# Linear attention and a GELU MLP on one core: outputs and state products of two chunks at a time, instead of outputs of four and states of four

## The chip, the cores and the metric

The kernel runs on one core of a Trainium2 chip. The core has five engines that work side by side and wait for each other through semaphores: TensorE (PE in the profile; PEld is its weight load), VectorE (DVE), ScalarE (ACT), GpSimd (POOL) and SyncE (SP), which here issues DMA transfers. The metric is the device time in microseconds (us), the median of several runs. The profile is of one execution.

## The reference

There are two stages. The first is linear attention with decay, over 4 batches, 8 heads, 768 positions and head dimension 64, in blocks of 64 positions:

```python
for b in range(nb):
    intra = einsum('bhic,bhjc->bhij', qb, kb) * Dmask          # lam ** (i - j), lower triangle
    intra = einsum('bhij,bhjd->bhid', intra, vb)
    inter = einsum('bhid,bhde->bhie', qb * lam_pow, kv_state)   # what earlier blocks left
    out[:, :, sl] = intra + inter
    kv_state = lam_block * kv_state + einsum('bhsd,bhse->bhde', kb * rev_pow, vb)
```

The second takes the attention's output as 3072 tokens of 512 features and computes gelu(x @ w_in) @ w_out, with 2048 hidden features and the exact GELU. Inputs and outputs are float32.

## The kernel before

The kernel computes in bf16 with float32 accumulation. It cuts the sequence into chunks of 128 positions, so there are 6 chunks for each of 4 batches, 24 in all. Chunk n belongs to batch n % 4 and to place n // 4 in the sequence. The four chunks of one place are a group; groups are numbered 0 to 5.

For one chunk the attention has these parts:

- `dma_transposes` (lines 184 to 190) gets the transposed k (`kT`) and q (`qT`). SP issues two transposing DMAs; POOL multiplies q by its decay (`q_hat`) between them. `request` calls it.
- `decay_k` (line 165) gives `k_dec`, k times the decay, on POOL.
- `scores` (line 192) makes 8 products of 64x128 weights on TensorE into two PSUM banks, and DVE multiplies them by the mask into `sc_m`.
- `inter` (line 220) makes 4 products of the carried state with `qT`, into the bank `o_ps`.
- `intra` (line 227) adds 8 products with weights of 128x64, two for each pair of heads, into the same bank. Then `o_ps` is copied to the group's tile `x_t`, from group 2 on by DVE.
- `next_state` (line 203) makes 4 products of `k_dec` and v into a bank `kv_ps`. DVE adds the old state (`tmp`, line 216) and multiplies by the decay (`state`, line 217). `take_state` makes that the current state. Group 5 has none.

The MLP of group g needs the x_t of all four of its chunks. It is a list of blocks, each of four products of 512 columns on TensorE: 16 blocks of the first product (`mm1`, line 263, 17 in group 1, where the last chunk's columns of the first four are a block of their own), with GELU on ACT, and then 16 blocks of the second (`mm2`, line 275), four for each chunk. After each chunk's fourth block ACT copies the sum to `o_sb` and SP sends it out (lines 280 and 281).

While the MLP of group g runs, the attention of group g + 1 is computed by visits to TensorE between the blocks. The dictionary `visits` says ahead of which block a visit stands. For groups 1 to 4 the loop at line 433 fills it in. For group g the chunks visited begin at n = (g + 1) * 4:

- `pair_a(n)` and `pair_a(n + 2)`: the scores of two chunks each, ahead of blocks a0 and a1.
- `quad_b(n)`: inter of four chunks, then intra of four, ahead of block b.
- `kv(n, ..., n + 3)`: the state products of four, ahead of block st.
- `requests(m)`: transposes and `k_dec` of chunks m and m + 1, and the loads of chunks m + 2 and m + 3.

The schedule is manual: every engine carries out its instructions in the order in which the code issues them, and waits only for data and for buffers. So `requests` takes no time on TensorE, and where it stands matters for what lies ahead of it on the queues of SP (output transfers and transposes) and of POOL (`q_hat`, `k_dec` and the issue of loads).

The tag "sc" has four PSUM banks, used in turn for scores, `o_ps` and `kv_ps`. The tag "m" has the other four, for the MLP. Chunks of q, k and v have 12 buffers each, `kT`, `qT`, `q_hat` and `sc_m` 6, `k_dec` 8, `o_sb` 6, `x_t` 2.

Of the kernel before, what the change touches and what calls it, by code (L numbers as in the profile page):

```python
# [9 lines left out]
BF16 = mybir.dt.bfloat16  # L10
# [5 lines left out]
def kernel(  # L16
# [12 lines left out]
    B, H, S, D = q.shape  # L29
# [10 lines left out]
    M = B  # L40
    NG = NB
# [7 lines left out]
    work_pool = ctx.enter_context(tc.tile_pool(name="work", bufs=6))  # L49
# [104 lines left out]
    live = {}  # L154

    def bank(shape, dtype, tag, name):
        return ps.tile(shape, dtype, tag=tag, name=name, bufs=4)
# [7 lines left out]
    def decay_k(c, eng):  # L165

        if c.so < NB - 1:
            c.k_dec = work_pool.tile([128, H, D], BF16, tag="kd", name="k_dec", bufs=8)
            eng.tensor_mul(c.k_dec, c.k, lam_m[:, :, None].to_broadcast((128, H, D)))  # L169

    def transposes(c, between=lambda: None):
# [20 lines left out]
    def scores(c):  # L192
        sc_ps = [bank([128, HP, C], F32, "sc", f"sc_ps{hi}") for hi in range(2)]
        for hp in range(HP):
            for hi in range(2):
                p = slice(hi * D, (hi + 1) * D)
                nc.tensor.matmul(sc_ps[hi][:, hp, :], c.kT[p, hp, :], c.qT[p, hp, :], start=True, stop=True)  # L197
        c.sc_m = work_pool.tile([128, HP, 2, C], BF16, tag="sc_m", name="sc_m")
        dmask_r = dmask.rearrange("p (hp hi) i -> p hp hi i", hi=2)
        for hi in range(2):  # L200
            nc.vector.tensor_mul(c.sc_m[:, :, hi, :], sc_ps[hi], dmask_r[:, :, hi, :])  # L201

    def next_state(c):

        if c.so == NB - 1:
            return
        kv_ps = bank([128, HP, 128], F32, "sc", "kv_ps")
        for hp in range(HP):
            nc.tensor.matmul(kv_ps[:, hp, :], c.k_dec[:, 2 * hp:2 * hp + 2, :], c.v[:, 2 * hp:2 * hp + 2, :],  # L209
                             start=True, stop=True)  # L210
        new = state_pool.tile([128, HP, 128], BF16, tag=f"state{c.b}", name="state")
        if c.so == 0:
            nc.vector.tensor_mul(new, kv_ps, lam_blk)
        else:
            tmp = state_pool.tile([128, HP, 128], F32, tag="tmp", name="tmp")
            nc.vector.tensor_add(tmp, kv_ps, states[c.b])  # L216
            nc.vector.tensor_mul(new, tmp, lam_blk)  # L217
        c.after = new

    def inter(c):  # L220
        c.o_ps = bank([128, HP, C], F32, "sc", "o_ps")
        if c.so > 0:
            for hp in range(HP):
                nc.tensor.matmul(c.o_ps[:, hp, :], states[c.b][:, hp, :], c.qT[:, hp, :],  # L224
                                 start=(hp == 0), stop=False, skip_group_check=True)

    def intra(c):
        for hp in range(HP):
            for hi in range(2):
                nc.tensor.matmul(c.o_ps[hi * D:(hi + 1) * D, hp, :], c.v[:, 2 * hp + hi, :], c.sc_m[:, hp, hi, :],  # L230
                                 start=(c.so == 0 and hp == 0), stop=True, skip_group_check=True)
        x_o = xT[c.so][:, :, c.b * C:(c.b + 1) * C]
        if c.so < 2:
            nc.scalar.copy(x_o, c.o_ps)
        else:
            nc.vector.tensor_copy(x_o, c.o_ps)  # L236
# [5 lines left out]
    def take_state(c):  # L242

        if c.so < NB - 1:
            states[c.b] = c.after
# [109 lines left out]
    for n in range(M):  # L355
        decay_k(live[n], nc.vector)
# [9 lines left out]
    def request(n):  # L366
        begin(n)
        dma_transposes(live[n])
# [3 lines left out]
    def prefetch(upto):  # L372
        while next_load[0] <= min(upto, NCH - 1):
            for name in "kqv":
                load(next_load[0], name)
            next_load[0] += 1

    def kv(*ns):
        for n in ns:
            next_state(live[n])  # L380
            take_state(live[n])

    def first_requests():
        for n in (2 * M, 2 * M + 1):
            request(n)
        for n in range(M, 2 * M):
            decay_k(live[n], nc.gpsimd)
        prefetch(2 * M + 3)
        for n in (2 * M, 2 * M + 1):
            decay_k(live[n], nc.gpsimd)  # L390
# [20 lines left out]
    def pair_a(n):  # L411
        for c in (live[n], live[n + 1]):
            scores(c)

    def quad_b(n):
        quad = [live[n + i] for i in range(M)]
        for c in quad:
            inter(c)
        for c in quad:
            intra(c)  # L420

    def requests(n):
        for m in (n, n + 1):
            request(m)
        for m in (n, n + 1):
            decay_k(live[m], nc.gpsimd)
        prefetch(n + 3)

    def add(g, i, f):
        visits.setdefault((g, i), []).append(f)  # L430


    for g in range(1, NG - 1):
        n = (g + 1) * M
        a0, a1, b, st = {1: (10, 22, 27, 31), 2: (6, 19, 25, 30)}.get(g, (5, 14, 21, 28))
        if g == 1:
            add(g, a0 - 2, lambda n=n: requests(n + 2))
        add(g, a0, lambda n=n: pair_a(n))
        add(g, a1, lambda n=n: pair_a(n + 2))
        if g + 2 < NG:  # L440
            add(g, a1 + 1, lambda n=n: requests(n + M))
            add(g, b + 1, lambda n=n: requests(n + M + 2))
        add(g, b, lambda n=n: quad_b(n))
        add(g, st, lambda n=n: kv(n, n + 1, n + 2, n + 3))

    for g in range(NG):
        if g + 1 < NG:
# [34 lines left out]
```

## Time and profile before

| what | us |
|---|---|
| median of 8 runs | 213.59 (213.04 to 214.54) |
| the profiled execution, its own time | 213.01 |
| its span, first to last instruction | 211.2 |
| PE busy | 205.9 |
| ACT / POOL / DVE busy | 87.3 / 102.8 / 75.8 |

The span lies inside the execution's own time, which is 1.8 us longer. A matmul's recorded length overlaps with the next one's, so busy time of PE says that it had work, not how much it got done; for that, start times are compared. The profile's first table gives busy time by engine, and a later one the chain of work that ended last. "L275" is line 275 of the kernel. In a time line, rows that follow each other on one engine with the same line are merged, and "x16" is their number.

### The profile page before, as it was taken

To read this page: it belongs to the slowest core of one execution; us is meant where nothing else is said; L and a number is where in the kernel's file an instruction comes from. 1 tells how busy PE (TensorE), PEld (TensorE's weight loads), DVE (VectorE), ACT (ScalarE), POOL (GpSimd) and SP (SyncE) were. 2 spreads that over 40 slices of the span, in tenths; PEclk is the share of its full clock that TensorE was granted. 3 is DMA by queue.
4 is the path that set the end of the run, shared out by engine and by line. 5 is a ranking of instruction groups with operands and counts; after the bars stand their busy time and mean duration, and the time that the engine had idled before them with its cause. 6 is when DMAs were issued, how large, how long until landed. Compare 5 with 4: busy or idle time off the path is not lost.

```text
span 211.2 us, 3570 instructions
## 1 busy us (share of the span) xinstructions
PE 205.9 (97%) x1472; PEld 105.5 (50%) x1472; DVE 75.8 (36%) x122; ACT 87.3 (41%) x153; POOL 102.8 (49%) x118
## 2 busy tenths in 40 slices
PE   7999999999999999999999999999999999999994
PEld 2545754556644455444465444455444464444442
DVE  3768130175393136740414842244542240000000
ACT  5674662326646111556211565311465311566121
POOL 7994533892997947949695295761000000000000
PEclk9999999999999999999999999999999999999999
DMA  7999999999999699999999969999400012100112
GB/s 86 134 158 197 206 207 188 155 209 154 179 91 117 78 164 111 145 129 175 98 150 116 160 140 147 111 161 119 149 0 0 3 50 99 50 3 0 50 50 99
DMA packets 100799, 24.48 MB, mean 116 GB/s; under 512 B 92976, under 2 KB 97840, under 8 KB 100784
## 3 DMA queue, kind: packets, MB, share of 16 engines
q0 software_dynamic: 78592, 13.51, 85.9%
q1 hardware_dynamic: 22192, 10.76, 25.1%
q8 instruction: 11, 0.18, 0.4%
q14 instruction: 4, 0.03, 0.1%
HBM read 27.27 MB, written 6.29 MB: 159 GB/s over the span
## 4 chain that ended last, share of the span: by engine, by line
PE 90%; DVE 5%; ACT 2%; DMA 1%; issue 1%
PE o_ps L275 38%; PE h_ps L263 38%; PE o_ps L230 3%; PE sc_ps L197 3%; PE o_ps L224 2%; PE kv_ps L209 2%; PE o_ps L289 2%; PE t_ps L176 2%; DVE state L217 1%; DMA lam_b<-in_lam_dram 1%; DVE tmp L216 1%; DVE sc_m L201 1%; PE idle_ps L324 1%; DVE qT L182 1%; ACT lam_q L132 1%
## 5 line engine op out<-in xcount | busy, mean ns | idle before, releaser
L263 PE MATMUL h_ps<-x_t,w_in_t 128*128 128x512 bf16 (+2 forms) x432 | 86.2, 356 | 0.0
L275 PE MATMUL o_ps<-w_out_t,g_t 128*128 128x512 bf16 x368 | 82.9, 379 | 0.0
L265 ACT ACTIVATE g_t<-h_ps 128x512 bf16<-128x512 f32 (+1 forms) x99 | 57.8, 584 | 34.0 <-PE h_ps L263 33.8
L263 PEld LDWEIGHTS <-w_in_t 128*128 128x128 bf16 x432 | 39.4, 98 | 41.6 <-DMA w_in_t<-in_moe_w_in_dram 0.3
L275 PEld LDWEIGHTS <-g_t 128*128 128x128 bf16 x368 | 35.0, 98 | 40.8
L201 DVE TENSOR_TENSOR sc_m<-sc_ps,dmask 128x512 bf16<-128x512 f32 x48 | 30.0, 683 | 41.2 <-PE sc_ps L197 41.2
L280 ACT COPY o_sb<-o_ps 128x512 f32<-128x512 f32 x23 | 13.5, 586 | 73.2 <-PE o_ps L275 73.2
L189 POOL TENSOR_TENSOR q_hat<-q_t,lam_p 128x512 bf16<-128x512 bf16 x16 | 17.2, 1073 | 28.4 <-issue 15.8
L66 POOL DMA_DIRECT2D k_t<-in_k_dram x24 | 22.1, 919 | 6.5 <-DMA w_in_t<-in_moe_w_in_dram 4.0
L66 POOL DMA_DIRECT2D q_t<-in_q_dram x24 | 21.6, 899 | 3.5 <-DMA w_out_t<-in_moe_w_out_dram 3.4
L66 POOL DMA_DIRECT2D v_t<-in_v_dram x23 | 20.8, 908 | 3.3 <-DMA w_out_t<-in_moe_w_out_dram 1.6
L236 DVE CAST x_t<-o_ps 128x512 bf16<-128x512 f32 x16 | 9.9, 684 | 18.1 <-PE o_ps L230 18.1
L169 POOL TENSOR_TENSOR k_dec<-k_t,lam_m 128x512 bf16<-128x512 bf16 x16 | 16.3, 1048 | 0.0
L216 DVE TENSOR_TENSOR tmp<-kv_ps,state 128x512 f32<-128x512 f32 x16 | 11.0, 685 | 12.4 <-PE kv_ps L209 12.4
L324 PE MATMUL idle_ps<-idle 128*128 128x512 bf16 x32 | 11.5, 476 | 1.2 <-DVE idle L105 1.2
L217 DVE TENSOR_TENSOR state<-tmp,lam_blk 128x512 bf16<-128x512 f32 x16 | 11.9, 746 | 0.6
L182 DVE TENSOR_TENSOR qT<-t_ps,lam_q 128x512 bf16<-128x512 bf16 x8 | 5.5, 690 | 14.9 <-PE t_ps L176 14.0
L197 PE MATMUL sc_ps<-qT,kT 64*128 64x128 bf16 x192 | 8.2, 217 | 0.8 <-DVE qT L182 0.4
L197 PEld LDWEIGHTS <-kT 64*128 64x128 bf16 x192 | 5.7, 94 | 6.4 <-issue 4.1
L230 PE MATMUL o_ps<-sc_m,v_t 128*64 128x128 bf16 x192 | 7.9, 222 | 0.2
L230 PEld LDWEIGHTS <-v_t 128*64 128x64 bf16 x192 | 5.8, 109 | 2.8 <-issue 1.6
L181 ACT COPY kT<-t_ps 128x512 bf16<-128x512 bf16 x8 | 4.7, 589 | 5.1 <-PE t_ps L176 5.1
(41 smaller groups left out, 71.6 us busy)
## 6 DMA issues: line engine op xcount, KB each, us to landing
out_dram<-o_sb SPq DMA_DIRECT2D x23, 256.0 KB, 2.3
k_t<-in_k_dram POOLq DMA_DIRECT2D x24, 128.0 KB, 4.6
q_t<-in_q_dram POOLq DMA_DIRECT2D x24, 128.0 KB, 5.7
v_t<-in_v_dram POOLq DMA_DIRECT2D x23, 128.0 KB, 6.6
w_out_t<-in_moe_w_out_dram POOLq DMA_DIRECT2D x4, 512.0 KB, 16.8
w_in_t<-in_moe_w_in_dram POOLq DMA_DIRECT2D x2, 512.0 KB, 11.3
w_in_t<-in_moe_w_in_dram POOLq DMA_DIRECT2D x2, 384.0 KB, 7.8
v_f<-in_v_dram SPq DMA_DIRECT2D x1, 256.0 KB, 3.6
```

Of the source, the lines that this page charges most:

```text
L66: nc.gpsimd.dma_start(raw[n, name], chunk_of(name, n))
L169: eng.tensor_mul(c.k_dec, c.k, lam_m[:, :, None].to_broadcast((128, H, D)))
L189: nc.gpsimd.tensor_mul(q_hat, c.q, lam_p[:, :, None].to_broadcast((128, H, D)))
L197: nc.tensor.matmul(sc_ps[hi][:, hp, :], c.kT[p, hp, :], c.qT[p, hp, :], start=True, stop=True)
L201: nc.vector.tensor_mul(c.sc_m[:, :, hi, :], sc_ps[hi], dmask_r[:, :, hi, :])
L217: nc.vector.tensor_mul(new, tmp, lam_blk)
L230: nc.tensor.matmul(c.o_ps[hi * D:(hi + 1) * D, hp, :], c.v[:, 2 * hp + hi, :], c.sc_m[:, hp, hi, :], start=(c.so == 0 and hp == 0), stop=T ...
L263: nc.tensor.matmul(h_ps[:, f, :], w, x_t[:, ki, lo:hi], start=(ki == 0 and f == 0), stop=(ki == NK1 - 1), skip_group_check=True)
L265: nc.scalar.activation(g_t[:, kf:kf + n_kf, lo:hi], h_ps, ACT.Gelu)
L275: nc.tensor.matmul(om[io], g_t[:, kf, io * C:(io + 1) * C], w_out_t[:, kf, :], start=(kf == 0), stop=(kf == NK2 - 1))
L280: nc.scalar.copy(o_sb, om[io])
L324: nc.tensor.matmul(idle_ps[0], idle[:, :128], idle, start=True, stop=True)
```

## The change

`quad_b` becomes `pair_b`. For two chunks it issues inter, then the state products, then intra and the taking over of the state. The separate kv visit is gone. Each group now has four visits in the order scores, `pair_b`, scores, `pair_b`, at the blocks (10, 15, 21, 27) in group 1 and (4, 10, 18, 26) in groups 2 to 4. Requests stand two blocks ahead of the first scores and one block after the first `pair_b`. `k_dec` takes the pool's 6 buffers instead of 8. The visits of group 0, the first ones of group 1 (up to block 7), the MLP and the loads of the weights are as they were.

```diff
     def decay_k(c, eng):
         if c.so < NB - 1:
-            c.k_dec = work_pool.tile([128, H, D], BF16, tag="kd", name="k_dec", bufs=8)
+            c.k_dec = work_pool.tile([128, H, D], BF16, tag="kd", name="k_dec")
...
-    def quad_b(n):
-        quad = [live[n + i] for i in range(M)]
-        for c in quad:
+    def pair_b(n):
+        pair = live[n], live[n + 1]
+        for c in pair:
             inter(c)
-        for c in quad:
+        for c in pair:
+            next_state(c)
+        for c in pair:
             intra(c)
+            take_state(c)
...
     for g in range(1, NG - 1):
         n = (g + 1) * M
-        a0, a1, b, st = {1: (10, 22, 27, 31), 2: (6, 19, 25, 30)}.get(g, (5, 14, 21, 28))
-        if g == 1:
-            add(g, a0 - 2, lambda n=n: requests(n + 2))
+        a0, b0, a1, b1 = (10, 15, 21, 27) if g == 1 else (4, 10, 18, 26)
+        add(g, a0 - 2, lambda n=n: requests(n + 2))
         add(g, a0, lambda n=n: pair_a(n))
+        add(g, b0, lambda n=n: pair_b(n))
+        if g + 2 < NG:
+            add(g, b0 + 1, lambda n=n: requests(n + M))
         add(g, a1, lambda n=n: pair_a(n + 2))
-        if g + 2 < NG:
-            add(g, a1 + 1, lambda n=n: requests(n + M))
-            add(g, b + 1, lambda n=n: requests(n + M + 2))
-        add(g, b, lambda n=n: quad_b(n))
-        add(g, st, lambda n=n: kv(n, n + 1, n + 2, n + 3))
+        add(g, b1, lambda n=n: pair_b(n + 2))
```

## The prediction

> **What bounds the kernel now.** I read the page first, then the stretches by group, then TensorE in order of time.
>
> ```profile
> span 211.2 us, 3570 instructions
> PE 205.9 (97%) x1472; PEld 105.5 (50%) x1472; DVE 75.8 (36%) x122; ACT 87.3 (41%) x153; POOL 102.8 (49%) x118
> PEclk9999999999999999999999999999999999999999
> PE 90%; DVE 5%; ACT 2%; DMA 1%; issue 1%
> ```
>
> TensorE is busy for 97% of the span, at full clock in all slices, and makes up 90% of the chain that ended last. Busy matmuls overlap, so this could hide slack. The table by stretch (groups 1 and 2 with the seams before them; its length comes after the stretch, then PE's busy time) says that there is next to none:
>
> ```profile
> 50.00:85.60 35.60, 35.47 (x293) 19.07 (x291) 17.59 (x27) 13.84 (x25) 28.72 (x31) 1.00 1.39 128
> 85.60:117.40 31.80, 31.80 (x225) 15.98 (x224) 12.66 (x21) 11.90 (x20) 23.17 (x25) 1.00 1.58 135
> ```
>
> Group 1's stretch has 0.13 us of idle, group 2's none. So what decides is how long each visit holds TensorE, and whether the new places make it wait. The time line of TensorE gives the first (start, length, line; the next row's start minus its own is what a row really holds the engine):
>
> ```profile
> 47.06 0.61 PE L224 MATMUL o_ps<-qT,state 128*128 128x128 bf16 x8
> 47.60 0.64 PE L230 MATMUL o_ps<-sc_m,v_t 128*64 128x128 bf16 x16
> 48.17 0.40 PE L197 MATMUL sc_ps<-qT,kT 64*128 64x128 bf16 x8
> ...
> 136.90 1.06 PE L224 MATMUL o_ps<-qT,state 128*128 128x128 bf16 x16
> 137.89 1.08 PE L230 MATMUL o_ps<-sc_m,v_t 128*64 128x128 bf16 x32
> 138.90 6.22 PE L275 MATMUL o_ps<-w_out_t,g_t 128*128 128x512 bf16 x28
> 144.96 1.06 PE L209 MATMUL kv_ps<-v_t,k_dec 128*128 128x128 bf16 x16
> 145.85 3.62 PE L275 MATMUL o_ps<-w_out_t,g_t 128*128 128x512 bf16 x16
> ```
>
> inter (L224): 8 hold 0.54, 16 hold 0.99: 0.45 per 8, and 0.09 fixed, paid on going over to intra. State products (L209): 16 hold 0.89, twice that 0.45 with nothing fixed. intra (L230): 16 hold 0.57, 32 hold 1.01: 0.44 per 16, and 0.13 fixed, paid on going in and back out to full-width products. So every change from full-width (128*128) to half-width weights (128*64) and back costs 0.22 us, and while it lasts nothing else runs on TensorE. An MLP product holds 6.06/28 = 0.216 us, a block of four 0.866.
>
> **The change, part by part.** (1) Each of groups 1 to 4 has one quad_b (16 inter, 32 intra) and, in groups 1 to 3, one kv visit of 16. It gets two pair_b, each 8 inter, 8 state products, 16 intra. No matmul is added. Before: 0.99 + 1.01 + 0.89 = 2.89 us per group, of which 0.22 is one change of width. After: the same streaming, 2.67, with two changes, 3.11. Group 4 has no state products: 2.00 becomes 2.22. The kv visit that disappears gives nothing back, since it had no fixed cost. Sum: 4 x 0.22 = +0.88 us, all on the path, since TensorE has no idle time to put it in. The going over from state products to intra is in no row. Its bounds: 0 if the state products in between hide it (0.09 less in each of 8 pair visits, 0.72 less in all), above the dearest change that the rows show, 0.13 (8 x 0.04 = 0.32 more). I take 0.09, since the state products have the form of inter (128*128, 128x128).
>
> Here the Trainium skill may be weighed. "TensorEngine Tiling (Array Packing)", section Key Properties, says that changing the tiling mode drains the TensorE, which the 0.22 us agrees with; it speaks against this change. With the drain of about 175 ns that "TensorE: Matmul & The Clock Gate", section Single matmul latency, gives, eight more changes (four in, four out) would be an estimated 1.4 us. The rows' 0.88 stands, since they have the same products.
>
> (2) DVE. Per pair its queue gets tmp, state, tmp, state, then the two copies to x_t, where before the copies came alone and the state work later.
>
> ```profile
> 57.11 1.23 DVE L217 TENSOR_TENSOR state<-tmp,lam_blk 128x512 bf16<-128x512 f32 x1
> ...
> 138.34 2.48 DVE L236 CAST x_t<-o_ps 128x512 bf16<-128x512 f32 x4 [5.13 <-PE o_ps L230]
> 145.38 0.69 DVE L216 TENSOR_TENSOR tmp<-kv_ps,state 128x512 f32<-128x512 f32 x1 [4.55 <-PE kv_ps L209]
> ...
> 146.72 0.68 DVE L216 TENSOR_TENSOR tmp<-kv_ps,state 128x512 f32<-128x512 f32 x1
> ```
>
> The first tmp starts 0.42 after its state products (145.38 against 144.96), so 0.87 into the visit; a chunk's tmp and state take 1.34 (146.72 - 145.38); the four copies took 2.48, 0.62 each. The last copy ends 0.87 + 2.68 + 1.24 = 4.8 us into the visit. Who waits for it: the scores that need the o_ps banks, and for the second pair the next group's first MLP product, which reads x_t. Both come 6 blocks after the visit at the earliest: 1.56 + 6 x 0.866 = 6.76. Slack 1.96, cost nothing. The cover thins where POOL multiplies beside it: the L217 at 57.11 took 1.23 instead of 0.69. With both slow the copy ends at 5.9, slack 0.9.
>
> The page "SBUF — State Buffer", section Who interferes with whom, goes further: a DVE instruction with two SBUF inputs and a GpSimd one that reads SBUF block each other fully. With a whole k_dec (1.05) behind each state, an estimate by it is 4.8 + 2.1 = 6.9 and a stall of 0.15 at a seam, at most 0.6 over four; no row shows more than 1.23.
>
> (3) New earliest dates for data. In group 1, block 10's products resume at 62.16, so b0 (block 15) begins at 62.16 + 5 x 0.866 = 66.49, its state products 0.45 later at 66.94; a1 begins at 66.49 + 6.76 = 73.25.
>
> ```profile
> 63.04 2.09 POOL L169 TENSOR_TENSOR k_dec<-k_t,lam_m 128x512 bf16<-128x512 bf16 x2
> ...
> 68.83 1.19 SPq L190 DMA_TRANSPOSE qT<-q_hat  x1
> ```
>
> ```profile
> qT<-q_hat SPq DMA_TRANSPOSE x1, 2.4
> ```
>
> k_dec of chunks 8 and 9 is done at 65.13, 1.8 us ahead; the last qT for a1 (issued 68.83, landed 2.4 later, the DMA view of that stretch) is there at 71.2, 2.0 ahead. Nothing on POOL's queue moves: its instructions keep their order. k_dec with 6 buffers instead of 8 waits for the state products of six chunks earlier: chunk 10's (POOL at 68.22) for chunk 4's, done by 57; chunk 14's (93.94) for chunk 8's, about 67.5; later ones have as much. Cost nothing.
>
> (4) SP's queue. The requests for chunks 12, 16 and 20 move ahead of a group's four output transfers, those for 14, 18 and 22 behind all four. The moved-back ones are the risk. Request 14 stands behind the out of group 1's last block (copied at 85.84 by ACT); its first transpose went out only at 87.59 before, so nothing changes. Request 18 can start at about 118; four transposes of 1.3 us each are issued by 123.2, and with the slowest landing that the kT row has (9.2) are there at 132.4, for a visit at 117.8 + 18 x 0.866 + 2.1 = 135.5. Request 22: 150.2, 155.4, 164.6, against 167.7. The moved-ahead ones hold outputs back (group 1's first, ready at 72.5, until 83.4); at most three pile up, for six buffers. Cost nothing. The loads of w_in are not in the diff: nothing.
>
> Sum against the profiled execution: 213.01 + 0.88 = 213.89. The median of the runs is 0.58 above that execution, so the forecast is 214.47, 0.41% more.
>
> **Rivals.**
> A: a new wait beside it. POOL's q_hat waited 3.30 and 1.09 us for loads before the k_dec of chunks 8 and 9, so these follow DMA, which is near full until 150 us. If POOL is later by more than 1.8 us, b0 waits, and what exceeds it is added: 1 us more gives 215.5. Likewise a seam of (2). Against it: every slack worked out is 0.9 us or more.
> B, the other side: the state products between inter and intra take over the drain, so that going in costs nothing. Then the 0.09 goes in all eight pair visits: 0.88 - 0.72 = +0.16, 213.75, no longer slower by 0.3% (0.64 us, about what a measurement of this kernel can tell from no change). It decides from 0.03 of the 0.09 hidden. Against it: inter, of the same form, hides nothing.
> C, faster: the one spell lost in these groups is in the first scores of group 1, which hold 0.89 us (61.27 to 62.16) where all later ones hold 0.55 (72.63 to 73.18); neither they nor what stands ahead of them is moved. Even if these 0.34 went, with B, it gives 213.4. Nothing in the profile could pay for 0.64.
>
> **How the numbers follow.** The forecast's case 0.76, A 0.12, B 0.10, C 0.02. The first is 0.24 us above the bound, and the eight runs shown spread by 1.5 us, so one in six of it may read as the same: slower 0.63 + 0.12 = 0.75, same 0.13 + 0.09 = 0.22, faster 0.03. The range is from B, 213.7, to A with 1 us and 0.1 of scatter, 215.6.
>
> **What would show it.** pair_b rows with L224 x8, L209 x8, L230 x16 holding 1.56 us; the change to L230 about 0.09; group 2's first product at 85.8, group 5's at 181.1 (180.26 before), the span 212.1; PE idle after 66 us nil. The forecast is wrong by A if PE waits for x_t's copies, k_dec or a transpose, and by B if L209 x8 holds 0.45, not 0.54.

## The result and the profile after

The changed kernel takes 214.43 us (median, 213.84 to 215.15), the kernel before, run beside it, 213.45 (212.74 to 214.86). The ratio is 1.0041, with a 95% interval of 1.0029 to 1.0053. The forecast was 214.47 and 0.41% more.

The profiled execution took 214.44 us, its span is 212.7. From the page of the changed kernel:

```profile
span 212.7 us, 3583 instructions
PE 206.1 (97%) x1472; PEld 105.2 (49%) x1472; DVE 77.2 (36%) x122; ACT 87.2 (41%) x153; POOL 104.3 (49%) x118
PEclk9999999999999999999999999999999999999999
PE 89%; DVE 4%; DMA 2%; POOL 2%; issue 0%; ACT 0%; POOLq 0%
```

In what it says of TensorE nothing tells the two kernels apart: as many matmuls, the same busy share, the same clock. DVE and POOL are busy for 1.4 and 1.5 us more, which the last section comes back to. The table by stretch (stretch and length, then PE's busy time, of groups 1 and 2 of the changed kernel):

```profile
50.00:85.80 35.80, 35.62 (x299) 19.43 (x297) 21.78 (x32) 14.26 (x25) 28.49 (x29) 1.00 1.38 119
85.80:117.90 32.10, 32.10 (x226) 16.04 (x225) 13.20 (x20) 11.90 (x20) 24.72 (x27) 1.00 1.53 149
```

TensorE has no idle time in group 2, as before. From 64 us on, no wait of TensorE is listed at all. So the time is not in waits. It is in what the visits hold. The time line of TensorE in the changed kernel, one pair visit with state products and one without:

```profile
79.62 0.61 PE L224 MATMUL o_ps<-qT,state 128*128 128x128 bf16 x8
80.07 0.61 PE L209 MATMUL kv_ps<-v_t,k_dec 128*128 128x128 bf16 x8
80.61 0.64 PE L230 MATMUL o_ps<-sc_m,v_t 128*64 128x128 bf16 x16
81.18 5.35 PE L275 MATMUL o_ps<-w_out_t,g_t 128*128 128x512 bf16 x24
...
159.82 0.61 PE L224 MATMUL o_ps<-qT,state 128*128 128x128 bf16 x8
160.36 0.64 PE L230 MATMUL o_ps<-sc_m,v_t 128*64 128x128 bf16 x16
160.93 5.35 PE L263 MATMUL h_ps<-x_t,w_in_t 128*128 128x512 bf16 x24
```

Start to start, inter holds 0.45 where state products follow, and 0.54 where intra follows directly. The state products hold 0.54, which is 0.45 and the 0.09 of the change of width. Intra holds 0.57. A pair visit is 1.56 us (81.18 - 79.62), in group 4 it is 1.11. The six and the two make 11.58. The three quads, the three state visits and the last quad of before made 3 x 2.89 + 2.01 = 10.68. The difference is 0.90, for 0.88 forecast, which is within the rounding of the rows. The 2.01 of group 4's quad is from the kernel before:

```profile
168.75 1.06 PE L224 MATMUL o_ps<-qT,state 128*128 128x128 bf16 x16
169.74 1.08 PE L230 MATMUL o_ps<-sc_m,v_t 128*64 128x128 bf16 x32
170.76 9.67 PE L275 MATMUL o_ps<-w_out_t,g_t 128*128 128x512 bf16 x44
```

The two spans differ by 1.5 us, which is more. 0.49 of it lies before the change begins to act: the first scores of group 1 start at 61.76 here and at 61.27 before, and up to there both kernels issue the same work to TensorE. In the start of the changed kernel's profile transposes waited for loads of q (twice 0.6 us, waits that the profile of before does not list). The rows, of the changed kernel first, then of the kernel before:

```profile
61.76 0.45 PE L197 MATMUL sc_ps<-qT,kT 64*128 64x128 bf16 x9
62.40 0.38 PE L197 MATMUL sc_ps<-qT,kT 64*128 64x128 bf16 x7 [0.18 <-DVE tmp L216]
62.71 4.49 PE L263 MATMUL h_ps<-x_t,w_in_t 128*128 128x512 bf16 x20
...
181.72 13.98 PE L263 MATMUL h_ps<-x_t,w_in_t 128*128 128x512 bf16 x64
```

```profile
61.27 0.96 PE L197 MATMUL sc_ps<-qT,kT 64*128 64x128 bf16 x16
62.16 6.22 PE L263 MATMUL h_ps<-x_t,w_in_t 128*128 128x512 bf16 x28
...
180.26 13.98 PE L263 MATMUL h_ps<-x_t,w_in_t 128*128 128x512 bf16 x64
```

From those scores to the first product of group 5 it is 119.96 us (61.76 to 181.72), before it was 118.99 (61.27 to 180.26): 0.97. It consists of the visits' 0.90 and of 0.06 more that those scores hold (0.95 against 0.89), and rounding.

### The profile page after: what moved, and what is told of

Read it like the earlier page. It is cut to its first block, busy times and chain, and to the rows that moved or that the text cites. A ratio compares the mean times of both kernels' runs of the same rounds, so it can differ in the third digit from the quotient of the medians.

```text
span 212.7 us, 3583 instructions
## 1 busy us (share of the span) xinstructions
PE 206.1 (97%) x1472; PEld 105.2 (49%) x1472; DVE 77.2 (36%) x122; ACT 87.2 (41%) x153; POOL 104.3 (49%) x118
## 4 chain that ended last, share of the span: by engine, by line
PE 89%; DVE 4%; DMA 2%; POOL 2%; issue 0%; ACT 0%; POOLq 0%
PE o_ps L275 38%; PE h_ps L263 38%; PE o_ps L230 3%; PE sc_ps L197 3%; DMA q_t<-in_q_dram 2%; PE o_ps L224 2%; PE kv_ps L209 2%; PE o_ps L289 2%; PE t_ps L176 1%; DVE state L217 1%; POOL k_t L66 1%; DVE tmp L216 1%; DVE sc_m L201 1%; POOL q_t L66 1%; DVE qT L182 1%
## 5 line engine op out<-in xcount | busy, mean ns | idle before, releaser
L169 POOL TENSOR_TENSOR k_dec<-k_t,lam_m 128x512 bf16<-128x512 bf16 x16 | 17.7, 1133 | 0.0
L217 DVE TENSOR_TENSOR state<-tmp,lam_blk 128x512 bf16<-128x512 f32 x16 | 13.2, 825 | 0.5
L324 PE MATMUL idle_ps<-idle 128*128 128x512 bf16 x32 | 10.9, 456 | 1.2 <-DVE idle L105 1.2
L230 PE MATMUL o_ps<-sc_m,v_t 128*64 128x128 bf16 x192 | 8.6, 223 | 0.2
```

## The experiments

Three theories. W, the prediction's: each change of TensorE from full-width to half-width weights and back costs 0.22 us, and nothing waits. V: what costs is breaking into the MLP's products, whatever the width. Q: the moved requests and the smaller pool for `k_dec` make the time, by way of SP, POOL and DMA. V counts the visits with intra alone: counted by visits of any kind, the two kernels differ only in group 4 (four against three), which at 0.22 a visit would not give the 0.9.

### The width of intra's weights, in both kernels

```diff
     def intra(c):
+        if c.so >= 2:
+            for hp in range(HP):
+                nc.tensor.matmul(c.o_ps[:, hp, :], c.v[:, 2 * hp:2 * hp + 2, :], c.sc_m[:, hp, 0, :],
+                                 start=False, stop=True, skip_group_check=True)
-        for hp in range(HP):
+        for hp in range(HP if c.so < 2 else 0):
             for hi in range(2):
```

> The kernel before, but intra of chunks 8 to 23 (all that is visited in groups 1 to 4) is one full-width product for a pair of heads, with the masked scores of the first head alone, in place of two half-width ones. This leaves the second head's scores out, so the output is not the reference's; the streaming is the same (4 x 0.056 us for a chunk). Theory W (each change of TensorE from full-width to half-width weights and back costs 0.22 us): one change less in each of four quad visits, 4 x 0.22 = 0.88 us less, 213.45 - 0.88 = 212.57, ratio 0.996. Theory V (a visit costs 0.22 for breaking into the MLP's products, whatever its width): 213.45, ratio 1.000. Theory Q (the moved requests and the smaller k_dec pool make the change slower, not TensorE): 213.45, 1.000.

> The changed kernel with the same full-width intra for chunks 8 to 23 (the second head's scores left out). W: eight changes less, 8 x 0.22 = 1.76 us less, 214.43 - 1.76 = 212.67, ratio to the kernel before 0.9963, and equal to the kernel before with full-width intra within 0.1 us. V: 214.4, ratio 1.004, 0.9 us above its partner. Q: the same 1.004, 0.9 above its partner.

Measured: the kernel before with full-width intra 212.51 us, ratio 0.9949 (0.9928 to 0.9969); the changed kernel with it 212.67 us, ratio 0.9953 (0.9935 to 0.9971). The difference between the two schedules is gone as far as these runs can tell: 0.16 us between the medians, where 0.98 was, with intervals of about 0.8 us. (W had expected 0.1 at most.) The number of visits and their places are those of the real kernels, so V and Q fall, both having asked for 0.9. The smaller number of products is not the cause either: both kernels lose the same 64 of intra's products, but the changed one gains 1.76 us by it (medians, 1.76 forecast) and the one before 0.94 (0.88 forecast), about twice as much for twice as many visits. The time lines, first of the quad in the kernel before with full-width intra (its added lines shift the line numbers of the MLP by four), then of a pair in the changed one:

```profile
136.61 1.06 PE L224 MATMUL o_ps<-qT,state 128*128 128x128 bf16 x16
137.50 1.06 PE L230 MATMUL o_ps<-sc_m,v_t 128*128 128x128 bf16 x16
138.39 6.21 PE L279 MATMUL o_ps<-w_out_t,g_t 128*128 128x512 bf16 x28
```

```profile
126.70 0.61 PE L224 MATMUL o_ps<-qT,state 128*128 128x128 bf16 x8
127.15 0.61 PE L209 MATMUL kv_ps<-v_t,k_dec 128*128 128x128 bf16 x8
127.60 0.61 PE L230 MATMUL o_ps<-sc_m,v_t 128*128 128x128 bf16 x8
128.04 5.34 PE L267 MATMUL h_ps<-x_t,w_in_t 128*128 128x512 bf16 x24
```

Sixteen inter hold 0.89 now, not 0.99, and sixteen full-width intra 0.89: no fixed part is left. The pair visit holds 1.34 instead of 1.56, the 0.22 that was predicted for one change and back.

### Twice as many changes of width

```diff
-    def pair_b(n):
-        pair = live[n], live[n + 1]
+    def one_b(n):
+        pair = live[n],
...
-        add(g, b0, lambda n=n: pair_b(n))
+        add(g, b0, lambda n=n: one_b(n))
+        add(g, b0 + 1, lambda n=n: one_b(n + 1))
...
-        add(g, b1, lambda n=n: pair_b(n + 2))
+        add(g, b1, lambda n=n: one_b(n + 2))
+        add(g, b1 + 1, lambda n=n: one_b(n + 3))
```

> The changed kernel with every pair visit cut into two visits of one chunk each, a block apart: 16 visits with inter, state products and intra in place of 8. W and V: eight more changes, 8 x 0.22 = 1.76 us more, 214.43 + 1.76 = 216.2, ratio 1.0128; no engine waits. Q: 214.4, ratio 1.004.

Measured: 216.35 us, ratio 1.0118 (1.0087 to 1.0150). The 1.0128 of W and V is inside, Q's 1.004 is not. The medians differ from the changed kernel's by 1.92, for 1.76 forecast. One visit on TensorE's time line:

```profile
69.76 0.39 PE L224 MATMUL o_ps<-qT,state 128*128 128x128 bf16 x4
69.98 0.39 PE L209 MATMUL kv_ps<-v_t,k_dec 128*128 128x128 bf16 x4
70.30 0.41 PE L230 MATMUL o_ps<-sc_m,v_t 128*64 128x128 bf16 x8
70.65 1.04 PE L263 MATMUL h_ps<-x_t,w_in_t 128*128 128x512 bf16 x4
```

It holds 0.89. Two of them are 1.78, 0.22 more than the pair's 1.56, for the same products.

### The requests and the buffers alone

```diff
-            c.k_dec = work_pool.tile([128, H, D], BF16, tag="kd", name="k_dec", bufs=8)
+            c.k_dec = work_pool.tile([128, H, D], BF16, tag="kd", name="k_dec")
...
-        if g == 1:
-            add(g, a0 - 2, lambda n=n: requests(n + 2))
+        r0, r1 = (8, 16) if g == 1 else (2, 11)
+        add(g, r0, lambda n=n: requests(n + 2))
...
-            add(g, a1 + 1, lambda n=n: requests(n + M))
-            add(g, b + 1, lambda n=n: requests(n + M + 2))
+            add(g, r1, lambda n=n: requests(n + M))
```

> The kernel before, visits as they were (quads and their state visits), but with the changed kernel's places for the requests and its 6 buffers for k_dec: the part of the change that TensorE does not carry out. W and V: 213.45, ratio 1.000. Q: all of the change, 214.4, ratio 1.004.

Measured: 213.56 us, ratio 0.9998 (0.9978 to 1.0017). This part of the change costs nothing that shows, as W expected: the interval goes from 0.5 us less to 0.4 more, and Q's 0.9 is outside.

### The state products behind intra

```diff
         for c in pair:
             inter(c)
         for c in pair:
-            next_state(c)
-        for c in pair:
             intra(c)
+        for c in pair:
+            next_state(c)
             take_state(c)
```

> The changed kernel with the state products behind intra in each pair visit instead of between inter and intra. W: as many changes of width, 214.4, ratio 1.004; inter x8 now goes over to intra with the same 0.09, L230 x16 holds 0.57. Theory H (the state products between hide part of the drain): inter to intra dearer than L209 to L230 in the changed kernel, up to 8 x 0.09 = 0.72 us more, 215.1, ratio 1.008.

Measured: 214.38 us, ratio 1.0044 (1.0027 to 1.0060), the changed kernel's own figure. Theory H, rival B seen from the other end, falls. A visit on TensorE's time line:

```profile
78.99 0.61 PE L224 MATMUL o_ps<-qT,state 128*128 128x128 bf16 x8
79.53 0.64 PE L230 MATMUL o_ps<-sc_m,v_t 128*64 128x128 bf16 x16
80.10 0.62 PE L209 MATMUL kv_ps<-v_t,k_dec 128*128 128x128 bf16 x8
80.56 2.75 PE L275 MATMUL o_ps<-w_out_t,g_t 128*128 128x512 bf16 x12
```

The 0.54 has moved from the state products to inter, the sum is 1.57, so no part of the going over is hidden in either order. intra still holds 0.57, though state products follow it and not the MLP: the way back is paid to what comes next at full width.

### A cover taken away

```diff
-        a0, b0, a1, b1 = (10, 15, 21, 27) if g == 1 else (4, 10, 18, 26)
+        a0, b0, a1, b1 = (10, 11, 21, 27) if g == 1 else (4, 10, 18, 26)
...
-            add(g, b0 + 1, lambda n=n: requests(n + M))
+            add(g, 16 if g == 1 else b0 + 1, lambda n=n: requests(n + M))
```

> The changed kernel with the first pair visit of group 1 ahead of block 11 instead of 15 (its requests stay ahead of block 16): the cover of that visit is taken away. By the changed kernel's trace it would begin at 62.71 + 0.87 = 63.6 and its second state products at 64.2, while the fourth sc_m that holds the last bank ends at 65.6 and k_dec of chunk 9 at 65.7. If the slacks were read rightly, TensorE waits there some 1.4 us, with DVE L201 or POOL L169 as the releaser, and nothing gives it back: 214.4 + 1.4 = 215.8, ratio 1.011. If the cover does not matter (work of theirs would move forward too): 214.4, ratio 1.004.

Measured: 215.55 us, ratio 1.0106 (1.0084 to 1.0127), as expected from the slacks. The time line of that visit (PEld rows left out):

```profile
62.73 2.47 DVE L201 TENSOR_TENSOR sc_m<-sc_ps,dmask 128x512 bf16<-128x512 f32 x4
63.18 2.10 POOL L169 TENSOR_TENSOR k_dec<-k_t,lam_m 128x512 bf16<-128x512 bf16 x2
...
63.46 0.38 PE L224 MATMUL o_ps<-qT,state 128*128 128x128 bf16 x4
...
64.06 0.38 PE L224 MATMUL o_ps<-qT,state 128*128 128x128 bf16 x4 [0.21 <-DVE sc_m L201]
...
64.66 0.38 PE L209 MATMUL kv_ps<-v_t,k_dec 128*128 128x128 bf16 x4 [0.21 <-DVE sc_m L201]
...
65.34 0.40 PE L209 MATMUL kv_ps<-v_t,k_dec 128*128 128x128 bf16 x4 [0.30 <-POOL k_dec L169]
...
66.24 2.12 PE L263 MATMUL h_ps<-x_t,w_in_t 128*128 128x512 bf16 x9
```

Each group of four waits for the next bank that DVE lets go, and the last for `k_dec`, done at 65.28. The visit holds 2.78 us (63.46, where its first inter starts, to 66.24) instead of 1.56, and that first inter starts 0.26 late besides (the block ahead of it began at 62.33 and holds 0.87). Together that is 1.48 us, for some 1.4 expected. The releasers are those that were expected. The prediction itself had worked out only the cover of `k_dec`; the banks that DVE's `sc_m` holds are a cover that it left out (in the changed kernel the fourth `sc_m` was done at 65.58, the state products began at 67.48). Once the cover is gone, the time is not given back.

### Group 1's first scores two blocks later, in the kernel before

```diff
-        a0, a1, b, st = {1: (10, 22, 27, 31), 2: (6, 19, 25, 30)}.get(g, (5, 14, 21, 28))
+        a0, a1, b, st = {1: (12, 22, 27, 31), 2: (6, 19, 25, 30)}.get(g, (5, 14, 21, 28))
         if g == 1:
-            add(g, a0 - 2, lambda n=n: requests(n + 2))
+            add(g, 8, lambda n=n: requests(n + 2))
```

> The kernel before with one number changed: group 1's first scores ahead of block 12 instead of 10 (their requests stay at 8). They held TensorE 0.89 us instead of 0.55, because DVE was still at the state work of chunks 6 and 7 that holds the banks. If that is why, the 0.34 us go: 213.45 - 0.34 = 213.1, ratio 0.998, and the scores there hold 0.55. If the wait has another cause that moves along, 213.45.

Measured: 213.12 us against 213.24 for the kernel before beside it, ratio 0.9989 (0.9975 to 1.0004). The interval holds both the 0.998 expected and no change, so this is not settled. In the profile the wait is gone, the scores hold 0.55:

```profile
63.54 0.62 PE L197 MATMUL sc_ps<-qT,kT 64*128 64x128 bf16 x16
64.09 2.12 PE L263 MATMUL h_ps<-x_t,w_in_t 128*128 128x512 bf16 x9
```

The wait does not always stand at this place. The same scores, with the same work ahead of them, hold 0.89 in the profile of before, 0.95 in the changed kernel, 1.14 with the requests alone moved, but 0.55 with the state products last and 0.56 in the changed kernel with full-width intra. In these last two TensorE had waited before it, 0.5 and 0.4 us in all, for POOL's `k_dec` at the state products of chunks 4 to 7. With the state products last these hold 0.68 and 0.72, where they hold 0.44 or 0.45 in the profiles of before and of the changed kernel. The time is lost a few us earlier there, not saved:

```profile
55.71 0.85 PE L209 MATMUL kv_ps<-v_t,k_dec 128*128 128x128 bf16 x8
56.39 1.89 PE L263 MATMUL h_ps<-x_t,w_in_t 128*128 128x512 bf16 x8
58.12 0.88 PE L209 MATMUL kv_ps<-v_t,k_dec 128*128 128x128 bf16 x8
58.84 2.75 PE L263 MATMUL h_ps<-x_t,w_in_t 128*128 128x512 bf16 x12
```

## Why the prediction was right, point by point

- The sum of (1), +0.88. Right in place and in size. The visits on TensorE hold 0.90 more in the profile, and the medians differ by 0.98, with an interval of the ratio that is 0.62 to 1.13 us. Taking away the change of width alone takes away the difference, as far as the runs can tell, and cutting the visits in two once more costs what the rate says (1.92 for 1.76, with an interval of about 1.3 us). This is shown, not only argued. That the median came out within 0.04 us of the forecast is partly luck: the difference is 0.98 instead of 0.88, and the kernel before took 213.45, where the forecast had built on 213.59.
- The cost of going over from state products to intra, taken as 0.09 between 0 less and 0.13: 0.09 (80.07 to 80.61, less 0.45). Rival B, that the products between hide it, is refuted here and by the run with the state products last.
- The kv visit that disappears gives nothing back. Right: full-width products that follow the MLP's hold 0.056 us each, where they do not wait: 0.45 for the eight of inter at 79.62, and 0.89 for the 16 state products of the kernel before at 144.96.
- The Trainium skill's rule that a change of tiling mode drains TensorE ("TensorEngine Tiling (Array Packing)", Key Properties) agrees with the runs with full-width intra: without the change of mode the fixed part is gone. The estimate of 1.4 us worked out from the drain of a single matmul was too high; the rows' price held.
- (2), the chain on DVE. The last copy was forecast to end 4.8 us into the visit, 5.9 with both state instructions slow. In the changed kernel the latest of those that the next group waits for ended at 5.15 (83.49 + 1.28 - 79.62), in time for the 6.76; the latest of all eight visits, for which only scores wait, ended at 5.29. Right that it costs nothing, and the 6.9 of a full mutual block was not reached. The lines, from DVE's time line:

```profile
82.55 1.02 DVE L217 TENSOR_TENSOR state<-tmp,lam_blk 128x512 bf16<-128x512 f32 x1
83.49 1.28 DVE L236 CAST x_t<-o_ps 128x512 bf16<-128x512 f32 x2
```

- (3), data for the earlier visits. `k_dec` of chunks 8 and 9 was done at 65.67 for state products at 67.48, 1.8 us ahead, as worked out. Rival A did not come: TensorE waits neither for `k_dec` nor for x_t's copies or a transpose. The run with the visit four blocks earlier shows that it was the cover that kept it away: without the cover it came. Rival C, a gain, did not come either.
- (4), SP's queue. Request 18's transposes began at 119.7 (118 forecast) and the last was issued at 123.7 (123.2), request 22's at 151.8 and 155.8 (150.2 and 155.4). Three outputs of group 1 had piled up and went out from 84.3 on, the fourth followed its copy at 87.2. One reading was wrong, without cost: request 14, of which the prediction says that nothing changes, had its first transpose at 91.2 instead of 87.6, since POOL issued the load of its k at 85.4 instead of 83.6 and it took longer to land. TensorE waited for none of it.
- The check points: group 2's first product at 85.8 came at 86.37, group 5's at 181.1 came at 181.72, the span 212.1 was 212.7. All are late by the same 0.6: 0.49 from the start, which the change does not touch, and 0.06 from the scores' wait. The step that made these dates absolute left the start's scatter out. The forecast of the median was not hurt by it.

## What to carry to other kernels

On an engine without idle time a schedule is priced by start-to-start distances in its own time line: take two rows of the same form and different count, and what does not grow with the count is the fixed cost of a visit. Products with the same weight shape as the stream around them could be moved and split here at no cost, those with another shape (here 128x64 among 128x128) should be gathered, since each trip to it was paid anew, 0.22 us each. A move on other queues was worth nothing as long as its cover was there, and the cover can be worked out from the same time line.

## What was not expected

Products of TensorE were as regular as clockwork, but the start was not: the first scores of group 1 began between 61.3 us (before) and 62.8 (the kernel with single visits), although nothing ahead of them differs for TensorE. What the profiles do list are waits for loads, none in that of before, 1.2 us for q in the changed kernel, 1.0 for q and 0.6 for the MLP's weights with single visits.

POOL's `k_dec` took 1.04 us for one before, but up to 1.49 in the changed kernel, where DVE's state work falls beside it: the two of chunks 10 and 11 took 2.94 us together, before 2.04. DVE's state instruction was at most 1.23 us before, 1.28 in the changed kernel and 1.56 with the early visit, against 0.69 alone. With the requests alone moved, and the visits as before, it was 1.47, so it seems to depend on what happens to fall together in one execution. The 1.23 that the prediction took as its worst was not the worst. From the changed kernel's time line:

```profile
68.63 0.86 DVE L217 TENSOR_TENSOR state<-tmp,lam_blk 128x512 bf16<-128x512 f32 x1
68.90 2.94 POOL L169 TENSOR_TENSOR k_dec<-k_t,lam_m 128x512 bf16<-128x512 bf16 x2
```
